# An mLSTM cell and a GELU feed-forward block: the up projection as pairs of 64-row halves of the TensorE array

## The chip, the cores and the metric

The kernel runs on one core of one Trainium2 chip. The metric is the device time of one execution in microseconds. The kernel before took 833.14 us (median of three runs, 832.2 to 833.54).

## What is computed

Two blocks in a row, all in float32 (the two weight matrices arrive in float64). The first is a recurrent cell over 768 tokens for 4 batches of 8 heads with 40 features each:

```python
for t in range(S):
    m_new = np.maximum(f_gate[:, :, t] + m, i_gate[:, :, t])
    f_stab = np.exp(f_gate[:, :, t] + m - m_new)
    i_stab = np.exp(i_gate[:, :, t] - m_new)
    m = m_new
    C = f_stab[..., None, None] * C + i_stab[..., None, None] * np.einsum('bhd,bhe->bhde', vt, kt)
    n = f_stab[..., None] * n + i_stab[..., None] * kt
    y[:, :, t] = sigmoid(o_gate[:, :, t]) * (C q_t) / np.maximum(np.abs(n . q_t), 1.0)
```

Its output, with the heads side by side (3072 tokens of 320 features), goes into the second block:

```python
h = x @ w_in                                  # (3072, 320) @ (320, 2048)
g = 0.5 * h * (1.0 + erf(h / sqrt(2)))
return g @ w_out                              # (3072, 2048) @ (2048, 320)
```

## The kernel before

The 768 tokens of a batch are cut into six chunks of 128. For each chunk the kernel runs a **cell stage** (`cell_steps`, line 265) on the four batches, which leaves the 320 features of 4 x 128 = 512 tokens transposed in `xT`, and then an **up stage** (`up_steps`, line 353) that multiplies `xT` by `w_in` and applies GELU. The **down** projection of a chunk (`down_steps`, line 363) is woven into the cell stage of the next chunk, one part of four matmuls after each cell step; the last chunk's runs alone at the end. `weave` (line 23) spreads such filling steps evenly between the steps of the main list, and each engine executes its instructions in the order in which the program issues them.

A cell stage has 16 steps, four per batch: `turn` transposes k and q (tile `pt`, copied out by ScalarE to `kT`, `qT`); `scores` multiplies them (`ps`) and updates the state (`pc`); `values` forms the output `y` on TensorE, VectorE and GpSimd; `turn_y` (line 337) transposes `y`.

*The 320 features* are three blocks of 128, 128 and 64. `turn_y` transposes each block into one tile `px`; VectorE copies two blocks into `xT` (line 342), ScalarE the third (line 343). One up step (one of 16 tiles of 128 columns of `w_in`) is three matmuls over the three blocks, accumulated in one bank `pu`, then one GELU (line 359). A float32 matmul appears in the trace as two passes, so an up stage has 16 x 3 x 2 = 96 passes. A pass of the third block uses 64 of the array's rows, the others 128.

*The heads* of a pair in `scores` (line 286) each use 64 rows, one the lower and one the upper half of the array, with a bank each.

*The weights* come in as bits of float64. `weight_steps` (line 193) cuts `w_in` into 12 pieces (four of 512 columns by three blocks) and `w_out` into 16. `convert` does one on ScalarE (Abs, line 222), GpSimd (lines 223 to 225) and VectorE (lines 227 to 234), and then fetches the piece after the next one. The `w_in` pieces are woven into the first cell stage, the `w_out` pieces into the first up stage.

*Ahead of every cell stage* `activations` (line 257) puts four exponentials and four sigmoids on ScalarE, behind the last GELU; `turn`'s copies stand behind them in the same queue. `distances` (line 246) prepares the exponents on VectorE and GpSimd during the up stage.

PSUM has eight banks here: two each for `tr` (`pt`, `px`), `sc` (`ps`), `h` (`ph`, `pf`, `pc`) and `mm` (`pu`, `po`).

Of the kernel before, what the change touches and what calls it, by code (L numbers as in the profile page):

```python
# [14 lines left out]
P = 128  # L15


# The upper halves of the float64 2^-126 and of the largest below 2^128, read as float32.
TINY = 3.4332275390625e-05
# [3 lines left out]
def weave(main, fill):  # L23
    """Run the steps of main in order with those of fill spread evenly between them."""
    done = 0
    for n, step in enumerate(main):
        step()
        upto = len(fill) * (n + 1) // len(main)
        for f in fill[done:upto]:
            f()  # L30
        done = upto
    for f in fill[done:]:
        f()
# [3 lines left out]
def kernel(  # L37
# [11 lines left out]
):  # L49
    # The cell in chunks of L tokens. With b_t the sum of f from the chunk's first token to t and  # L50
    # a_s = i_s - b_s, the stabiliser is m_t = b_t + M_t, M_t = max(m before the chunk, a_s for s <= t), and
    #   (C_t, n_t) = exp(m_before - M_t) (C, n)_before + sum over s <= t of exp(a_s - M_t) (v_s, 1) k_s^T.
    # Every exponent is at most 0, so this holds for gates of any size.
    nc = tc.nc
# [11 lines left out]
    TG = B * L  # L66
    KX = DM - 2 * P
    NLD = 6
    NM = 3
    WP = 512  # L70
    assert S % L == 0 and DFF % P == 0 and 0 < KX <= P and D <= DP and NLD > B

# [6 lines left out]
    ps_tr = ctx.enter_context(tc.tile_pool(name="ps_tr", bufs=2, space=bass.MemoryType.PSUM))  # L79
    ps_sc = ctx.enter_context(tc.tile_pool(name="ps_sc", bufs=2, space=bass.MemoryType.PSUM))  # L80
    ps_h = ctx.enter_context(tc.tile_pool(name="ps_h", bufs=2, space=bass.MemoryType.PSUM))
    ps_mm = ctx.enter_context(tc.tile_pool(name="ps_mm", bufs=2, space=bass.MemoryType.PSUM))
    gate_ctx = ExitStack()
    gates = gate_ctx.enter_context(tc.tile_pool(name="gates", bufs=1))
    ctx.enter_context(tc.manual_schedule())

    # ---- what stays: weights, state, load buffers with their constant parts
    w_in = const.tile([P, 3, DFF], F32, name="w_in")
    w_out = const.tile([P, NF, DM], F32, name="w_out")
    ident = const.tile([P, P], F32, name="ident")  # L90
    last = const.tile([P, P], F32, name="last")
    xT = const.tile([P, 3, TG], F32, name="xT")
    aT = const.tile([P, NCH, BH], F32, name="aT")
# [12 lines left out]
    def load(n):  # L106
        """The inputs of token tile n (chunk n // B of batch n % B), one token a partition."""
        if n >= NCH * B:
            return
        c, b = divmod(n, B)  # L110
        for src, dst in ((q, qb), (k, kb), (v, vb), (o_gate, ob)):
            nc.sync.dma_start(out=dst[n % NLD][:, :, 0:D],
                              in_=src[b, :, c * L:(c + 1) * L, :].rearrange("h p d -> p h d"))
# [3 lines left out]
    def load_M(n):  # L117
        """M of token tile n on every partition."""
        if n >= NCH * B:
            return  # L120
        c, b = divmod(n, B)
        Mb[n] = wts.tile([P, H, L], F32, name="Mb", tag="Mb", bufs=NM)
        nc.sync.dma_start(out=Mb[n], in_=M_d[b * H:(b + 1) * H, c * L:(c + 1) * L]
                          .unsqueeze(0).to_broadcast([P, H, L]))
# [19 lines left out]

    # ---- the gates, one row a head
    keep = gates.tile([BH, NCH, L], F32, name="keep")
# [38 lines left out]

    # ---- the weights come in float64: the nearest float32, from the bits
    w_src = {}
# [5 lines left out]
    def weight_steps():  # L193
        """What brings w_in and w_out in, a piece of at most WP columns a step."""
        pieces = []
        for f0 in range(0, DFF, WP):
            for cc, w in enumerate((P, P, KX)):
                pieces.append((w_src["in"][cc * P:cc * P + w, 2 * f0:2 * f0 + 2 * WP], w_in[0:w, cc, f0:f0 + WP]))
        n_in = len(pieces)
        for f in range(NF):  # L200
            pieces.append((w_src["out"][f * P:(f + 1) * P, :], w_out[:, f, :]))
        loaded = {}

        def fetch(i):
            if i < len(pieces):
                src, dst = pieces[i]
                w, n = dst.shape
                t = raw.tile([P, WP, 2], U32, name="bits", tag="bits")
                loaded[i] = t[0:w, 0:n, :]
                nc.sync.dma_start(out=loaded[i].rearrange("p n two -> p (n two)"), in_=src)  # L210

        def convert(i):
            dst = pieces[i][1]
            w, n = dst.shape
            x = loaded.pop(i)
            lo, hi = x[:, :, 0], x[:, :, 1]
            hf = hi.bitcast(F32)
            s = raw.tile([P, WP], F32, name="sig", tag="sig")[0:w, 0:n]
            p = raw.tile([P, WP], F32, name="pow", tag="pow")[0:w, 0:n]
            su, pu = s.bitcast(U32), p.bitcast(U32)  # L220
            # Into the range of float32: 0 below 2^-126, the end of the range from 2^128 on.
            nc.scalar.activation(out=s, in_=hf, func=AF.Abs)  # L222
            nc.gpsimd.tensor_scalar(out=s, in0=s, scalar1=TINY, scalar2=None, op0=OP.is_ge)  # L223
            nc.gpsimd.tensor_tensor(out=s, in0=s, in1=hf, op=OP.mult)  # L224
            nc.gpsimd.tensor_scalar(out=s, in0=s, scalar1=-HUGE, scalar2=HUGE, op0=OP.max, op1=OP.min)  # L225
            # The sign and the power of two, and the 53 bits of the significand rounded to 24.
            nc.vector.tensor_scalar(out=pu, in0=su, scalar1=3, scalar2=0x3F800000,  # L227
                                    op0=OP.logical_shift_left, op1=OP.bitwise_and)
            nc.vector.scalar_tensor_tensor(out=pu, in0=su, scalar=0xC0000000, in1=pu,
                                           op0=OP.bitwise_and, op1=OP.bitwise_or)  # L230
            nc.vector.tensor_scalar(out=su, in0=su, scalar1=0xFFFFF, scalar2=0x100000,
                                    op0=OP.bitwise_and, op1=OP.bitwise_or)
            nc.vector.scalar_tensor_tensor(out=s, in0=lo, scalar=2.0 ** -32, in1=su, op0=OP.mult, op1=OP.add)
            nc.vector.scalar_tensor_tensor(out=dst, in0=s, scalar=2.0 ** -20, in1=p, op0=OP.mult, op1=OP.mult)
            fetch(i + 2)
# [5 lines left out]

    # ---- the cell
    def per_head(t, c, b):
        return t[:, c, b * H:(b + 1) * H].unsqueeze(2)

    def distances(c):
        """M_t - a_s for the chunk's weights exp(a_s - M_t); beyond the diagonal, what gives 0."""
        for b in range(B):
# [16 lines left out]
    def cell_steps(c):  # L265
# [12 lines left out]
        def scores(b):  # L278
            n = c * B + b
            Pm[b] = W.pop(n)  # L280
            # The heads of a pair run side by side in the array: each has its own bank.
            ps = [ps_sc.tile([P, NP, L], F32, name="ps", tag="sc") for hip in range(2)]
            for p in range(NP):
# [33 lines left out]
        def values(b):  # L317
# [7 lines left out]
            else:  # L325
                nc.vector.tensor_copy(out=hs, in_=ph)
            ys[b] = two.tile([P, H, D], F32, name="y", tag="y")
            nc.gpsimd.tensor_tensor(out=ys[b], in0=hs[:, :, 0:D], in1=ob[n % NLD], op=OP.mult)  # L328
            den = two.tile([P, H], F32, name="den", tag="den")
# [3 lines left out]
            nc.vector.reciprocal(out=den, in_=den)  # L333
            nc.vector.tensor_tensor(out=ys[b], in0=ys[b], in1=den.unsqueeze(2).to_broadcast([P, H, D]), op=OP.mult)
            load(n + NLD)

        def turn_y(b):
            y = ys[b].rearrange("p h d -> p (h d)")
            px = ps_tr.tile([P, 3, L], F32, name="px", tag="tr")
            for cc, w in enumerate((P, P, KX)):  # L340
                nc.tensor.transpose(px[0:w, cc, :], y[:, cc * P:cc * P + w], ident)  # L341
            nc.vector.tensor_copy(out=xT[:, 0:2, b * L:(b + 1) * L], in_=px[:, 0:2, :])
            nc.scalar.copy(out=xT[0:KX, 2, b * L:(b + 1) * L], in_=px[0:KX, 2, :])

# [6 lines left out]

    # ---- the feed-forward block, on the tokens of one chunk of every batch
    def up_steps(g):
        def step(f):
            m = slice(f * P, (f + 1) * P)
            pu = ps_mm.tile([P, TG], F32, name="pu", tag="mm")
            for cc, w in enumerate((P, P, KX)):
                nc.tensor.matmul(pu, w_in[0:w, cc, m], xT[0:w, cc, :], start=(cc == 0), stop=(cc == 2))  # L358
            nc.scalar.activation(out=g[:, f, :], in_=pu, func=AF.Gelu)  # L359

        return [lambda f=f: step(f) for f in range(NF)]

# [62 lines left out]
```

## Time and profile before

| | |
|---|---|
| Median of three runs | 833.14 us |
| Span of the profiled execution | 830.5 us |
| TensorE matmul busy | 674.7 us (81%) |
| VectorE, ScalarE, GpSimd busy | 240.7, 170.4, 199.5 us |
| Mean granted TensorE clock | 0.910 |
| One up stage, chunks 1 to 5 | 47.3 us |

The span runs from the first to the last instruction; the 2.6 us between it and the median of the runs lie outside of the profile. The matmul busy time counts passes whose ends are modelled and overlap, so a busy TensorE says where the engine has work, not how fast it could be. The rate is read from the starts of passes that follow each other.

### The profile page before, as it was taken

How to read it: one execution, taken by the hardware profiler on the slowest of the kernel's cores; microseconds unless marked ns; L12 is line 12 of the kernel's file. 1: busy time of each engine (PE TensorE's matmuls, PEld its weight loads, DVE VectorE, ACT ScalarE, POOL GpSimd, SP SyncE). 2: the span in 40 equal slices, each digit the busy share in tenths (PEclk: the TensorE clock that was granted, in tenths of full speed). 3: DMA queues.
4: the chain of work that ended last, by engine and by line, in shares of the span. 5: the costliest groups of instructions: out<-in, count | busy, mean ns of one | idle time of the engine just before them, and what ended most of it. 6: DMA issues, size and time to landing. Idle time of an engine off the chain costs nothing.

```text
span 830.5 us, 7094 instructions
## 1 busy us (share of the span) xinstructions
PE 674.7 (81%) x2714; PEld 394.8 (48%) x2714; DVE 240.7 (29%) x438; ACT 170.4 (21%) x288; POOL 199.5 (24%) x214
## 2 busy tenths in 40 slices
PE   2136424477579999799999799997999997999998
PEld 1125321122258733388533587333885335773365
DVE  4257554455534320034400144200344001330000
ACT  1411002111330022510223300225102234012200
POOL 2276654766612130011300021300113000000000
PEclk9975556788879999999999899998999998999999
DMA  9944371522204540024500035400221000000000
GB/s 141 248 80 95 66 120 29 148 64 63 63 9 66 79 110 0 0 41 66 133 23 1 6 64 82 109 0 1 41 40 41 1 0 9 9 17 0 0 9 24
DMA packets 132208, 43.47 MB, mean 52 GB/s; under 512 B 101104, under 2 KB 128752, under 8 KB 132176
## 3 DMA queue, kind: packets, MB, share of 16 engines
q1 hardware_dynamic: 132176, 43.04, 25.7%
q8 instruction: 21, 0.34, 0.2%
q14 instruction: 11, 0.09, 0.0%
HBM read 38.99 MB, written 4.03 MB: 52 GB/s over the span
## 4 chain that ended last, share of the span: by engine, by line
PE 67%; POOL 13%; issue 11%; ACT 5%; DVE 1%; DMA 1%; SPq 0%; POOLq 0%; ACTq 0%
PE pu L358 28%; PE po L371 25%; POOL sig L225 4%; PE ph L321 4%; POOL sig L223 4%; POOL sig L224 3%; PE ps L286 3%; PE pf L293 3%; ACT W L260 2%; PE pt L273 2%; PE pc L305 2%; POOL W L253 1%; ACT ob L263 1%; PE px L341 1%; ACT L263 1%
## 5 line engine op out<-in xcount | busy, mean ns | idle before, releaser
L358 PE MATMUL pu<-xT,w_in 128*128 128x512 f32 (+1 forms) x576 | 296.2, 646 | 36.4 <-ACT g L359 20.8
L371 PE MATMUL po<-w_out,g 128*128 128x320 f32 x768 | 228.5, 445 | 0.0
L358 PEld LDWEIGHTS pu<-xT,w_in 128*128 128x128 f32 (+1 forms) x576 | 96.6, 193 | 233.2 <-issue 189.8
L371 PEld LDWEIGHTS po<-w_out,g 128*128 128x128 f32 x768 | 143.6, 196 | 51.2 <-issue 5.0
L289 DVE TENSOR_TENSOR W<-ps,W 128x512 f32<-128x512 f32 x48 | 30.9, 685 | 293.5 <-PE ps L286 293.5
L359 ACT ACTIVATE g<-pu 128x512 f32<-128x512 f32 x96 | 57.1, 594 | 187.2 <-PE pu L358 187.2
L314 POOL TENSOR_TENSOR state<-state,dec 64x164 f32<-64x164 f32 x32 | 14.7, 461 | 241.5 <-PE pf L293 240.3
L273 PE MATMUL pt<-ident,kb 128*128 128x128 f32 x96 | 19.2, 335 | 60.5 <-ACT kT L276 60.5
L328 POOL TENSOR_TENSOR y<-hs,ob 128x320 f32<-128x320 f32 x24 | 19.3, 805 | 189.0 <-DVE hs L324 164.8
L321 PEld LDWEIGHTS ph<-vb,W 128*128 128x128 f32 x384 | 53.0, 215 | 4.0 <-PE px L341 0.8
L321 PE MATMUL ph<-vb,W 128*128 128x41 f32 x384 | 51.7, 300 | 0.4 <-PE px L341 0.4
L305 PE MATMUL pc<-vw,kb 128*128 128x82 f32 x160 | 24.9, 306 | 32.2 <-POOL vw L300 32.2
L253 POOL TENSOR_SCALAR_AFFINE_SELECT W<-W 128x1024 f32<-128x1024 f32 x24 | 37.2, 1571 | 56.9 <-DVE W L251 56.9
L273 PEld LDWEIGHTS pt<-ident,kb 128*128 128x128 f32 x96 | 14.1, 173 | 69.3 <-ACT kT L276 63.5
L223 POOL TENSOR_SCALAR sig<-sig 128x320 f32<-128x320 f32 (+2 forms) x28 | 34.8, 1243 | 47.0 <-ACT sig L222 47.0
L225 POOL TENSOR_SCALAR sig<-sig 128x320 f32<-128x320 f32 (+2 forms) x28 | 44.3, 1582 | 2.5
L251 DVE TENSOR_TENSOR W<-Mb,aT 128x1024 f32<-128x1024 f32 x24 | 33.3, 1425 | 26.0 <-DMA Mb<-M_d 26.0
L227 DVE TENSOR_SCALAR pow<-sig 128x320 uint32<-128x320 uint32 (+2 forms) x28 | 15.2, 543 | 86.3 <-POOL sig L225 86.2
L305 PEld LDWEIGHTS pc<-vw,kb 128*128 128x128 f32 x160 | 22.7, 219 | 33.3 <-POOL vw L300 33.3
L374 ACT COPY o_sb<-po 128x320 f32<-128x320 f32 x24 | 10.2, 425 | 132.3 <-PE po L371 132.3
L276 ACT COPY kT<-pt 128x512 f32<-128x512 f32 x24 | 13.9, 579 | 106.5 <-PE pt L273 106.5
L222 ACT ACTIVATE sig<-bits 128x320 f32<-128x320 f32 (+2 forms) x28 | 15.6, 563 | 97.4 <-DMA bits<-in_moe_w_out_dram 66.3
(71 smaller groups left out, 453.9 us busy)
## 6 DMA issues: line engine op xcount, KB each, us to landing
Mb<-M_d SPq DMA_DIRECT2D x24, 512.0 KB, 5.3
bits<-in_moe_w_out_dram SPq DMA_DIRECT2D x16, 320.0 KB, 2.9
bits<-in_moe_w_in_dram SPq DMA_DIRECT2D x8, 512.0 KB, 3.8
qb<-in_q_dram SPq DMA_DIRECT2D x24, 160.0 KB, 4.1
kb<-in_k_dram SPq DMA_DIRECT2D x24, 160.0 KB, 4.2
vb<-in_v_dram SPq DMA_DIRECT2D x24, 160.0 KB, 4.2
ob<-in_o_gate_dram SPq DMA_DIRECT2D x24, 160.0 KB, 3.8
out_dram<-o_sb SPq DMA_DIRECT2D x24, 160.0 KB, 1.9
```

The costliest lines, as they stand in the source:

```text
L223: nc.gpsimd.tensor_scalar(out=s, in0=s, scalar1=TINY, scalar2=None, op0=OP.is_ge)
L224: nc.gpsimd.tensor_tensor(out=s, in0=s, in1=hf, op=OP.mult)
L225: nc.gpsimd.tensor_scalar(out=s, in0=s, scalar1=-HUGE, scalar2=HUGE, op0=OP.max, op1=OP.min)
L251: nc.vector.tensor_tensor(out=W[n], in0=Mb.pop(n), in1=per_head(aT, c, b).to_broadcast([P, H, L]), op=OP.subtract)
L253: nc.gpsimd.affine_select(out=W[n], in_=W[n], compare_op=OP.is_ge, fill=1.0e4, base=0, pattern=[[0, H], [1, L]], channel_multiplier=-1)
L273: nc.tensor.transpose(pt[:, p, :], src[n % NLD][:, 2 * p:2 * p + 2, :].rearrange("p h d -> p (h d)"), ident)
L289: nc.vector.tensor_tensor(out=w, in0=ps[hip], in1=w, op=OP.mult)
L305: nc.tensor.matmul(pc[:, p, :], kb[n % NLD][:, m, :].rearrange("p h d -> p (h d)"), vw[:, m, :].rearrange("p h d -> p (h d)"), start=True, ...
L321: nc.tensor.matmul(ph[:, h, :], Pm[b][:, h, :], vb[n % NLD][:, h, :], start=True, stop=True)
L358: nc.tensor.matmul(pu, w_in[0:w, cc, m], xT[0:w, cc, :], start=(cc == 0), stop=(cc == 2))
L359: nc.scalar.activation(out=g[:, f, :], in_=pu, func=AF.Gelu)
L371: nc.tensor.matmul(po, g[:, f, b * L:(b + 1) * L], w_out[:, f, :], start=(f == 0), stop=(f == NF - 1))
```

## The change

The 320 features become five blocks of 64. Two up tiles are done at a time, as a pair: the even tile's five matmuls use the lower 64 rows of the array, the odd tile's the upper 64, in turn, each into a bank of its own. For that the rows of `w_in` are laid out anew: a piece now holds one block of 64 rows, for even tiles on partitions 0 to 63 and for odd ones on 64 to 127, so there are ten pieces of 128 partitions and each is fetched by two DMAs. `xT` needs every block on both halves of the partitions: `y` is extended by a copy of its first 64 columns (a new VectorE copy), and `turn_y` makes five transposes of 128 columns at a step of 64, in two tiles `px`, so that block k lands on the lower and block k + 1 on the upper partitions. VectorE copies the lower halves, ScalarE the upper ones, two copies each. The pool of `ps` is dissolved; `ps`, `pu` and `po` share four banks.

```diff
+    R = P // 2
+    NK = DM // R
-    ps_sc = ctx.enter_context(tc.tile_pool(name="ps_sc", bufs=2, space=bass.MemoryType.PSUM))
-    ps_mm = ctx.enter_context(tc.tile_pool(name="ps_mm", bufs=2, space=bass.MemoryType.PSUM))
+    ps_mm = ctx.enter_context(tc.tile_pool(name="ps_mm", bufs=4, space=bass.MemoryType.PSUM))
-    w_in = const.tile([P, 3, DFF], F32, name="w_in")
+    w_in = const.tile([P, NK, DFF // 2], F32, name="w_in")
-    xT = const.tile([P, 3, TG], F32, name="xT")
+    xT = const.tile([P, NK, TG], F32, name="xT")
...
-        for f0 in range(0, DFF, WP):
-            for cc, w in enumerate((P, P, KX)):
-                pieces.append((w_src["in"][cc * P:cc * P + w, 2 * f0:2 * f0 + 2 * WP], w_in[0:w, cc, f0:f0 + WP]))
+        for f0 in range(0, DFF, 2 * WP):
+            for k in range(NK):
+                src = w_src["in"][k * R:(k + 1) * R, 2 * f0:2 * (f0 + 2 * WP)]
+                src = src.rearrange("k (m two x) -> k m two x", two=2, x=2 * P)
+                pieces.append(([(slice(R * e, R * e + R), src[:, :, e, :]) for e in range(2)],
+                               w_in[:, k, f0 // 2:f0 // 2 + WP]))
...
-                nc.sync.dma_start(out=loaded[i].rearrange("p n two -> p (n two)"), in_=src)
+                for r, src in parts:
+                    to = loaded[i][r].rearrange("p n two -> p (n two)")
+                    if len(src.shape) == 3:
+                        to = to.rearrange("p (m x) -> p m x", x=2 * P)
+                    nc.sync.dma_start(out=to, in_=src)
...
-            ps = [ps_sc.tile([P, NP, L], F32, name="ps", tag="sc") for hip in range(2)]
+            ps = [ps_mm.tile([P, NP, L], F32, name="ps", tag="mm") for hip in range(2)]
...
-            ys[b] = two.tile([P, H, D], F32, name="y", tag="y")
+            ys[b] = two.tile([P, DM + R], F32, name="y", tag="y")
...
+            nc.vector.tensor_copy(out=ys[b][:, DM:DM + R], in_=ys[b][:, 0:R])
...
-            px = ps_tr.tile([P, 3, L], F32, name="px", tag="tr")
-            for cc, w in enumerate((P, P, KX)):
-                nc.tensor.transpose(px[0:w, cc, :], y[:, cc * P:cc * P + w], ident)
-            nc.vector.tensor_copy(out=xT[:, 0:2, b * L:(b + 1) * L], in_=px[:, 0:2, :])
-            nc.scalar.copy(out=xT[0:KX, 2, b * L:(b + 1) * L], in_=px[0:KX, 2, :])
+            for k0, n in ((0, 3), (3, 2)):
+                px = ps_tr.tile([P, n, L], F32, name="px", tag="tr")
+                for k in range(n):
+                    nc.tensor.transpose(px[:, k, :], ys[b][:, (k0 + k) * R:(k0 + k + 2) * R], ident)
+                t = slice(b * L, (b + 1) * L)
+                nc.vector.tensor_copy(out=xT[0:R, k0:k0 + n, t], in_=px[0:R])
+                nc.scalar.copy(out=xT[R:P, k0:k0 + n, t], in_=px[R:P])
...
-            m = slice(f * P, (f + 1) * P)
-            pu = ps_mm.tile([P, TG], F32, name="pu", tag="mm")
-            for cc, w in enumerate((P, P, KX)):
-                nc.tensor.matmul(pu, w_in[0:w, cc, m], xT[0:w, cc, :], start=(cc == 0), stop=(cc == 2))
-            nc.scalar.activation(out=g[:, f, :], in_=pu, func=AF.Gelu)
+            pu = [ps_mm.tile([P, TG], F32, name="pu", tag="mm") for e in range(2)]
+            for k in range(NK):
+                for e in range(2):
+                    r = slice(R * e, R * e + R)
+                    nc.tensor.matmul(pu[e], w_in[r, k, f // 2 * P:(f // 2 + 1) * P], xT[r, (k - e) % NK, :],
+                                     start=(k == 0), stop=(k == NK - 1))
+            for e in range(2):
+                nc.scalar.activation(out=g[:, f + e, :], in_=pu[e], func=AF.Gelu)
-        return [lambda f=f: step(f) for f in range(NF)]
+        return [lambda f=f: step(f) for f in range(0, NF, 2)]
```

TensorE at the end of the cell stage of chunk 1, from the last `turn_y` into the up stage, before (`px` are the transposes of `y`, `po` a down part, `pu` the up matmuls; what stands in brackets are the engines that a row waits for):

```order
L341 MATMUL px<-ident,y 128x128 [waits DVE_49,Activation_49]
L341 MATMUL px<-ident,y 128x128
L341 MATMUL px<-ident,y 64x128
L371 MATMUL po<-w_out,g 128x320 x4
L358 MATMUL pu<-xT,w_in 128x512 [waits DVE_49]
L358 MATMUL pu<-xT,w_in 128x512
L358 MATMUL pu<-xT,w_in 128x512 [waits Activation_49] x2
```

The same place in the changed kernel:

```order
L356 MATMUL px<-ident,y 128x128 [waits Activation_49]
L356 MATMUL px<-ident,y 128x128 x2
L356 MATMUL px<-ident,y 128x128 [waits Activation_49]
L356 MATMUL px<-ident,y 128x128
L392 MATMUL po<-w_out,g 128x320 x4
L377 MATMUL pu<-xT,w_in 128x512 [waits DVE_49]
L377 MATMUL pu<-xT,w_in 128x512 [waits Activation_49]
L377 MATMUL pu<-xT,w_in 128x512 x4
```

Two transposes more stand in the step, the two `px` tiles each wait for ScalarE, and the second up matmul (the first on the upper half) waits for ScalarE, whose copy into `xT` it reads.

ScalarE in the first cell stage, before (`sig<-bits` is the Abs that begins the conversion of a piece, `kT` and `qT` are the copies of `turn`):

```order
L222 ACTIVATE sig<-bits 128x512 [waits DMAHW2_49]
L222 ACTIVATE sig<-bits 128x512 [waits DMAHW3_49]
L276 COPY kT<-pt 128x512 [waits PE_49,Activation_49]
L276 COPY qT<-pt 128x512 [waits PE_49,Activation_49]
L222 ACTIVATE sig<-bits 64x512 [waits DMAHW4_49,DVE_49]
```

The same place in the changed kernel:

```order
L233 ACTIVATE sig<-bits 128x512 [waits DMAHW3_49,DMAHW2_49]
L287 COPY kT<-pt 128x512 [waits PE_49,Activation_49]
L287 COPY qT<-pt 128x512 [waits PE_49,Activation_49]
L233 ACTIVATE sig<-bits 128x512 [waits DMAHW5_49,DMAHW4_49]
L233 ACTIVATE sig<-bits 128x512 [waits DMAHW7_49,DMAHW6_49,DVE_49]
```

With ten pieces instead of twelve spread over the 16 steps, the second piece's Abs has moved behind the copies of the third `turn`.

## Rows read from the trace of the kernel before

**Rows 1.** The page: the chain that ended last, shares of the span by engine.

```profile
PE 67%; POOL 13%; issue 11%; ACT 5%; DVE 1%; DMA 1%; SPq 0%; POOLq 0%; ACTq 0%
```

**Rows 2.** Busy us by engine in two stretches: chunk 2's and chunk 0's up stage.

```profile
core 0: us, PE busy (x) PEld busy (x) DVE busy (x) ACT busy (x) POOL busy (x), PEclk, DMA share, GB/s
405.40:452.60 47.20, 47.20 (x97) 15.29 (x95) 3.78 (x3) 10.66 (x17) 6.35 (x5) 1.00 0.17 48
...
142.00:226.00 84.00, 56.38 (x104) 18.61 (x102) 45.09 (x80) 15.99 (x31) 54.78 (x50) 0.83 0.29 84
```

**Rows 3.** The chain in order of time (start us, us, what): an up stage, last down.

```profile
405.36 47.28 PE pu L358 x96
...
792.61 34.66 PE po L371 x128
```

**Rows 4.** Timeline, TensorE: starts of five successive passes inside chunk 2's up stage.

```profile
429.79 1.02 PE L358 MATMUL pu<-xT,w_in 128*128 128x512 f32 x2
...
430.22 1.22 PE L358 MATMUL pu<-xT,w_in 128*128 128x512 f32 x2
...
430.74 1.12 PE L358 MATMUL pu<-xT,w_in 64*128 64x512 f32 x2
...
431.27 1.22 PE L358 MATMUL pu<-xT,w_in 64*128 64x512 f32 x2
...
431.79 1.13 PE L358 MATMUL pu<-xT,w_in 128*128 128x512 f32 x2
```

**Rows 5.** Timeline, TensorE: a scores step (64-row halves in turn) and transposes.

```profile
467.50 1.16 PE L286 MATMUL ps<-qT,kT 64*128 64x128 f32 x16
468.59 1.12 PE L293 MATMUL pf<-state,qT 128*128 128x82 f32 x8
...
472.64 0.60 PE L273 MATMUL pt<-ident,kb 128*128 128x128 f32 x4
473.07 0.60 PE L273 MATMUL pt<-ident,qb 128*128 128x128 f32 x4
```

**Rows 6.** Timeline, all engines: the last turn_y and the next up stage's start.

```profile
517.92 2.32 PE L371 MATMUL po<-w_out,g 128*128 128x320 f32 x8
...
518.58 0.26 ACT L343 COPY xT<-px 64x128 f32<-64x128 f32 x1 [2.23 <-DVE xT L342]
...
520.08 3.56 PE L358 MATMUL pu<-xT,w_in 128*128 128x512 f32 x7
```

**Rows 7.** Timeline, all engines: from an up stage's end into the cell stage.

```profile
452.67 0.60 ACT L359 ACTIVATE g<-pu 128x512 f32<-128x512 f32 x1 [2.37 <-PE pu L358]
453.28 1.28 ACT L260 ACT_TABLE_LOAD   x1
...
461.85 1.11 PE L273 MATMUL pt<-ident,kb 128*128 128x128 f32 x4 [6.04 <-ACT kT L276]
```

**Rows 8.** Timeline, all engines: conversions of w_in pieces in the first cell stage.

```profile
46.70 1.67 POOL L223 TENSOR_SCALAR sig<-sig 128x512 f32<-128x512 f32 x1
...
50.58 0.58 ACT L276 COPY qT<-pt 128x512 f32<-128x512 f32 x1 [0.26 <-PE pt L273]
...
118.57 1.50 POOL L223 TENSOR_SCALAR sig<-sig 128x512 f32<-128x512 f32 x1
...
125.84 0.69 DVE L234 SCALAR_TENSOR_TENSOR w_in<-sig,pow 128x512 f32<-128x512 f32 x1
...
126.45 0.41 DVE L342 COPY xT<-px 128x256 f32<-128x256 f32 x1
...
127.80 1.49 POOL L223 TENSOR_SCALAR sig<-sig 128x512 f32<-128x512 f32 x1 [4.36 <-ACT sig L222]
...
144.26 0.68 DVE L234 SCALAR_TENSOR_TENSOR w_in<-sig,pow 64x512 f32<-64x512 f32 x1
```

**Rows 9.** Timeline: one round of two w_out pieces in chunk 0's up stage.

```profile
203.00 9.30 PE L358 MATMUL pu<-xT,w_in 128*128 128x512 f32 x12 [2.13 <-ACT g L359]
...
211.95 0.49 ACT L222 ACTIVATE sig<-bits 128x320 f32<-128x320 f32 x1 [6.72 <-DMA bits<-in_moe_w_out_dram]
```

More of the change, by code (lines that the diff above doesn't have):

```diff
@@ L66 @@
     TG = B * L
-    KX = DM - 2 * P
+    R = P // 2
+    NK = DM // R
     NLD = 6
@@ L70 @@
     WP = 512
-    assert S % L == 0 and DFF % P == 0 and 0 < KX <= P and D <= DP and NLD > B
+    assert S % L == 0 and DFF % (2 * P) == 0 and DM % R == 0 and D <= DP and NLD > B
     const = ctx.enter_context(tc.tile_pool(name="const", bufs=1))
@@ L195, in weight_steps @@
         pieces = []
-        for f0 in range(0, DFF, WP):
-            for cc, w in enumerate((P, P, KX)):
-                pieces.append((w_src["in"][cc * P:cc * P + w, 2 * f0:2 * f0 + 2 * WP], w_in[0:w, cc, f0:f0 + WP]))
+        for f0 in range(0, DFF, 2 * WP):
[4 more added lines that the diff above has]
+                               w_in[:, k, f0 // 2:f0 // 2 + WP]))
         n_in = len(pieces)
         for f in range(NF):
-            pieces.append((w_src["out"][f * P:(f + 1) * P, :], w_out[:, f, :]))
+            pieces.append(([(slice(0, P), w_src["out"][f * P:(f + 1) * P, :])], w_out[:, f, :]))
         loaded = {}
@@ L205, in fetch @@
             if i < len(pieces):
-                src, dst = pieces[i]
-                w, n = dst.shape
+                parts, dst = pieces[i]
+                n = dst.shape[1]
                 t = raw.tile([P, WP, 2], U32, name="bits", tag="bits")
-                loaded[i] = t[0:w, 0:n, :]
-                nc.sync.dma_start(out=loaded[i].rearrange("p n two -> p (n two)"), in_=src)
+                loaded[i] = t[:, 0:n, :]
+                for r, src in parts:
[3 more added lines that the diff above has]
+                    nc.sync.dma_start(out=to, in_=src)
         def convert(i):
             dst = pieces[i][1]
-            w, n = dst.shape
+            n = dst.shape[1]
             x = loaded.pop(i)
@@ L217, in convert @@
             hf = hi.bitcast(F32)
-            s = raw.tile([P, WP], F32, name="sig", tag="sig")[0:w, 0:n]
-            p = raw.tile([P, WP], F32, name="pow", tag="pow")[0:w, 0:n]
+            s = raw.tile([P, WP], F32, name="sig", tag="sig")[:, 0:n]
+            p = raw.tile([P, WP], F32, name="pow", tag="pow")[:, 0:n]
             su, pu = s.bitcast(U32), p.bitcast(U32)
@@ L326, in values @@
                 nc.vector.tensor_copy(out=hs, in_=ph)
-            ys[b] = two.tile([P, H, D], F32, name="y", tag="y")
-            nc.gpsimd.tensor_tensor(out=ys[b], in0=hs[:, :, 0:D], in1=ob[n % NLD], op=OP.mult)
+            ys[b] = two.tile([P, DM + R], F32, name="y", tag="y")
+            y = ys[b][:, 0:DM].rearrange("p (h d) -> p h d", d=D)
+            nc.gpsimd.tensor_tensor(out=y, in0=hs[:, :, 0:D], in1=ob[n % NLD], op=OP.mult)
             den = two.tile([P, H], F32, name="den", tag="den")
@@ L333, in values @@
             nc.vector.reciprocal(out=den, in_=den)
-            nc.vector.tensor_tensor(out=ys[b], in0=ys[b], in1=den.unsqueeze(2).to_broadcast([P, H, D]), op=OP.mult)
+            nc.vector.tensor_tensor(out=y, in0=y, in1=den.unsqueeze(2).to_broadcast([P, H, D]), op=OP.mult)
+            nc.vector.tensor_copy(out=ys[b][:, DM:DM + R], in_=ys[b][:, 0:R])
             load(n + NLD)
         def turn_y(b):
-            y = ys[b].rearrange("p h d -> p (h d)")
-            px = ps_tr.tile([P, 3, L], F32, name="px", tag="tr")
-            for cc, w in enumerate((P, P, KX)):
-                nc.tensor.transpose(px[0:w, cc, :], y[:, cc * P:cc * P + w], ident)
-            nc.vector.tensor_copy(out=xT[:, 0:2, b * L:(b + 1) * L], in_=px[:, 0:2, :])
-            nc.scalar.copy(out=xT[0:KX, 2, b * L:(b + 1) * L], in_=px[0:KX, 2, :])
+            for k0, n in ((0, 3), (3, 2)):
[5 more added lines that the diff above has]
+                nc.scalar.copy(out=xT[R:P, k0:k0 + n, t], in_=px[R:P])
         steps = []
```

## The prediction

> **What bounds the kernel now.** I began with the chain of work that ended last: two thirds of the span are TensorE passes [rows 1], and in order of time they are, in chunks 1 to 5, an up stage of 96 passes in 47.28 us between cell stages in which the passes stand close together too; after the last up stage comes the last down projection [rows 3]. So a pass that becomes shorter in an up stage of chunks 1 to 5 moves the end. ScalarE works 10.66 us of those 47.2 and VectorE less, at a granted clock of 1.00 [rows 2]; they have room. Chunk 0 differs: its up stage lies in 84 us of which GpSimd works 54.78 and TensorE waits [rows 2]. There the conversions of the weights set the time, and a faster TensorE gives nothing.
>
> Next I read the rate inside an up stage, from the starts of passes that follow each other [rows 4]. A 128-row pass starts 0.43 us after the one before (429.79, 430.22). Into the 64-row block, inside it and out of it the steps are 0.52, 0.53 and 0.52 us. Six passes at 0.429 would be 2.57 us; a tile takes 47.28 / 16 = 2.955. So 0.38 us a tile goes where the array changes between 128 and 64 rows, and a 64-row pass of 512 columns costs as much as a full one.
>
> **What halves side by side do.** The only 64-row halves in turn are in the scores: 16 passes of 128 columns, and the next matmul starts 1.09 us after the first of them [rows 5]. Full passes of 128 columns start every 0.43 / 4 = 0.109 us (the transposes, 472.64 to 473.07 [rows 5]), so 16 in a row would be 1.74 us, and eight pairs at once 0.87. The 0.22 over is about one change of rows in and out. The halves do run side by side there, loading their weights too.
>
> **The up stages of chunks 1 to 5.** A pair of tiles is five blocks by two halves by two passes, ten pairs of passes; a stage has 80 pairs. At 0.429 us a pair, as for any pass of 512 columns [rows 4], that is 34.3 us, and 0.2 for the one change of rows at the stage's start: 34.5. Against 47.28 each stage saves 12.8, five save 63.9. Bounds: if I give the start-up of the scores to each pair, 1.09 / 8 = 0.136 against 0.109, a pair of 512 columns takes 0.535 and a stage 42.8; that the halves don't overlap at all is the slow rival. I take 0.429, since the scores' excess has the size of one change of rows and these come once a stage now.
>
> The Trainium skill (TensorE: Matmul & The Clock Gate, section Measured speedup vs the span model) reports that four row tiles of 32 rows with 512 columns gave 3.07 times, not 4. By that share two tiles would give 1.54, an estimate from that page; a pair would take 0.56 us and a stage 44.6, and the kernel would come out near 822 us. The scores show 1.6 with the change of rows in it, and no run here shows 512 columns.
>
> **Behind an up stage.** Exponentials, sigmoids and `turn`'s copies follow the last GELU on ScalarE, and TensorE waits 6.04 us for them [rows 7]. Both tiles of the last pair end together, so two GELUs instead of one stand ahead: +0.60 us [rows 7] at each of four boundaries (chunks 1 to 4; behind chunk 0 an Abs is last, behind chunk 5 the down parts run on), +2.4.
>
> **The cell stages.** `turn_y` has five transposes instead of three: 2 x 0.109 us, four batches, five stages in which TensorE is the chain: +4.4. The copies into `xT` grow: VectorE from one of 256 columns (0.41 us [rows 8]) to two of 384 and 256, ScalarE from one of 128 (0.26 [rows 6]) to two of the same widths, between 0.26 and the 0.58 of 512 columns [rows 8]. ScalarE waits for VectorE's copy before as well [rows 6]. From the first tile's end this is about 0.6 + 0.1 + 0.5 + 0.1 + 0.5 = 1.8 us, an estimate. Ahead of the up stage a down part covers it: 517.92 to 520.08, 2.16 us [rows 6], and the first `px` ends 0.2 earlier still. So 0.5 is left, and I count nothing; without that cover it would be up to 1.8 a stage. VectorE's copy of 64 columns of `y` costs at most the 0.41 of 256 columns and lies behind the same parts. The scores' banks now come from the shared pool: a `ps` can wait for ScalarE's copy of a `po`, but that `po` ended some steps before; nothing again.
>
> **The weights.** A late piece goes round alone: GpSimd from 118.57, VectorE until 125.84 + 0.69 = 126.53, the `xT` copies, Abs, and GpSimd begins the next at 127.80 [rows 8]: 9.23 us a piece. Two pieces fewer would be 18.5 us. But the order changes. The second piece ran directly behind the first, from 46.70; now its Abs stands behind `qT` of the third `turn`, which ended at 50.58 + 0.58 = 51.16 [rows 8], so it begins near 51.9. Further on, fewer pieces run back to back on GpSimd, and each turn of `turn_y` adds some 0.6 of copies. I went through the ten in their new order with the 7.96 us from GpSimd's first to VectorE's last operation, two more where GpSimd goes on to the next piece at once: GpSimd begins at about 41, 52, 57, 68, 74, 88, 100, 110, 123 and 133, and the last `w_in` operation ends near 140.4 instead of 144.94 [rows 8]. I take -4.5, with bounds of -18.5 (all that two pieces take) and 0 (the new order eats it all). Each fetch being two DMAs of shorter runs should hide, since in my walk the bits are there before Abs's turn.
>
> The `w_out` pieces stay 16, in rounds of two whose length is set by fetch, Abs, GpSimd and VectorE. The GELUs, now two by two, fall into the wait of 6.72 us before the next Abs [rows 9], and a pair of tiles at half the clock takes some 8.6 us against a round's 9 to 10. Nothing changes there but the start.
>
> **The sum.** -63.9 + 2.4 + 4.4 - 4.5 = -61.6. The profiled execution's span of 830.5 becomes 768.9; with the 2.6 us that lie outside of it, 771.5 us against the median of 833.14.
>
> **The rivals.** *The reload shows in every pair* (A): the 64-row passes of 512 columns in this trace are 0.53 apart [rows 4], and if that is the half array's own pace and not the change of rows, a stage is 80 x 0.533 = 42.6 us, five save 23.2, and the time is 833.1 - 23.2 + 2.3 = 812. For it: no 64-row pass of that width went faster. Against it: the step into the block is longer by as much, and the scores' passes keep pace. The page's share of 3.07 in 4, told above, would be a milder form of this rival and stands in its chance.
>
> *The halves take turns* (B), so that the change does not do what it says: two streams of 512 columns into two banks might not go at once. Then a stage is 160 x 0.429 = 68.6 us, five lose 106.7, and the time is 942. It decides from a pair of 0.585 us on, where the stage's gain equals the other terms. Against it stand the scores, where two banks take in both halves.
>
> *The covers fail* (C): each `turn_y` waits for its copies, since both tiles `px` now wait for ScalarE, which waits for VectorE, behind `values`. At 1.8 us each, 20 times, that is 36 us, and the time is 807. Against it: between two turns lies at least a down part of 2.16 us [rows 6].
>
> **How the numbers follow.** Forecast 82%, A 8%, B 4%, C 6%. The forecast's own range: down to 757.5 with all 18.5 us of the weights; up by 4.5 if these give nothing, by 4.8 if a pair takes 0.441 (2.5% slower than a lone pass), by 5 for waits of a microsecond in five stages: 786. That holds about eight in ten, and I keep 758 to 786. A measurement of this kernel tells 0.2%, or 1.7 us, from no change. Faster by more takes the forecast, A and C, 95%; slower is B, 4%; 1% is left between.
>
> **What would show it.** The up stages of chunks 1 to 5 should be one run of 160 passes in 34.5 us, starts in twos, 0.43 us apart. 42 to 43 us would be A, over 60 B. Idle time of TensorE ahead of `px` or of the first up matmuls, released by ScalarE's `xT` copy, would be C. The wait behind an up stage should grow from 6.0 to 6.6 us, the last VectorE operation on `w_in` end near 140, and chunk 0's up stage keep its rounds of nearly 10 us. The forecast is wrong above all if the pair's pace is.

## The result, and the profile after

The changed kernel takes 770.16 us (median of four runs, 768.05 to 770.72) against 832.9 us for the kernel before (median of four runs as well). The ratio of the two is 0.9248, with a 95% interval of 0.9231 to 0.9265. The profiled execution has a span of 768.9 us, 61.6 us less than before. The forecast was 771.5 us, with a span of 768.9. In every execution of these runs whose time and span are both on record, 1.7 to 1.9 us lie outside of the span; the 2.6 us that stand ahead and in the forecast also hold the difference between the profiled execution and the median. So the spans are the better comparison.

The chain of work that ended last, in order of time (start us, us, what), shows the up stages of chunks 1, 2 and 5 and the last down projection; these lines answer to [rows 3]:

```profile
289.09 34.58 PE pu L377 x160
...
392.25 34.58 PE pu L377 x160
...
696.55 34.53 PE pu L377 x160
731.08 34.66 PE po L392 x128
```

An up stage has 160 passes instead of 96, and 34.58 us instead of 47.28. The reason stands in the starts of passes inside the stage of chunk 2 (timeline, TensorE: start us, us, what, count of passes that touch a short window):

```profile
399.58 1.02 PE L377 MATMUL pu<-xT,w_in 64*128 64x512 f32 x4
...
400.01 0.60 PE L377 MATMUL pu<-xT,w_in 64*128 64x512 f32 x2
...
400.44 0.60 PE L377 MATMUL pu<-xT,w_in 64*128 64x512 f32 x2
```

Two passes begin together, and the next two 0.43 us later. That is the step that a single 128-row pass had in [rows 4], and the steps of 0.52 and 0.53 are gone. So two 64-row passes of 512 columns, one on each half, cost what one pass of 128 rows costs.

The boundary behind an up stage (timeline of ScalarE and TensorE; brackets: idle before it, and what ended it) answers to [rows 7]:

```profile
426.82 1.08 ACT L380 ACTIVATE g<-pu 128x512 f32<-128x512 f32 x2 [3.21 <-PE pu L377]
427.92 1.28 ACT L271 ACT_TABLE_LOAD   x1
429.21 3.89 ACT L271 ACTIVATE W<-W 128x1024 f32<-128x1024 f32 x4
...
436.49 1.11 PE L284 MATMUL pt<-ident,kb 128*128 128x128 f32 x4 [6.52 <-ACT kT L287]
```

Two GELUs stand before the exponentials where one stood, and TensorE's wait has grown from 6.04 to 6.52 us.

The last `turn_y` of a cell stage answers to [rows 6]:

```profile
389.39 0.71 PE L356 MATMUL px<-ident,y 128*128 128x128 f32 x5
389.92 0.88 DVE L358 COPY xT<-px 64x384 f32<-64x384 f32 x2 [1.82 <-PE px L356]
389.93 2.32 PE L392 MATMUL po<-w_out,g 128*128 128x320 f32 x8
390.50 0.74 ACT L359 COPY xT<-px 64x384 f32<-64x384 f32 x2 [1.96 <-DVE xT L358]
...
392.18 1.56 PE L377 MATMUL pu<-xT,w_in 64*128 64x512 f32 x6
```

ScalarE's second copy ends at 390.50 + 0.74 = 391.24, and the up stage begins at 392.18 without a wait: the down part between them covers the four copies. In chunks 1 to 5 TensorE never waits ahead of `px`; it waits there for ScalarE's copy twice in the first cell stage (6.01 and 11.03 us), where the conversions of the weights set the pace.

In the first cell stage the round of `w_in` pieces is the walk's, 0.5 to 1.3 us late (timeline; these answer to [rows 8]):

```profile
41.34 0.67 ACT L233 ACTIVATE sig<-bits 128x512 f32<-128x512 f32 x1 [0.71 <-DMA bits<-in_moe_w_in_dram]
...
52.76 1.50 POOL L234 TENSOR_SCALAR sig<-sig 128x512 f32<-128x512 f32 x1 [5.09 <-ACT sig L233]
...
133.54 1.50 POOL L234 TENSOR_SCALAR sig<-sig 128x512 f32<-128x512 f32 x1 [5.11 <-ACT sig L233]
...
140.83 0.69 DVE L245 SCALAR_TENSOR_TENSOR w_in<-sig,pow 128x512 f32<-128x512 f32 x1
```

The second piece begins at 52.76 (it was 46.70 before, and about 52 in the walk), the last at 133.54 (walk: 133), and the last operation on `w_in` ends at 141.52 (before 144.94, walk 140.4). The very first Abs now waits 0.71 us for its bits; before it did not. Chunk 0's up stage keeps its rounds: towards its end the first Abs of a round begins at 198.52, 208.30 and 218.06, every 9.8 us.

Term by term, from the starts of the up stages and of chunk 1's first transposes in both chains of work:

| Term | Forecast, us | Measured, us |
|---|---|---|
| Five up stages | -63.9 | -63.5 |
| Weights, up to chunk 1's first transposes (233.31 before, 229.43 after) | -4.5 | -3.9 |
| Cell stage of chunk 1 | +0.9 | +1.4 |
| Four boundaries with the cell stages behind them (chunks 2 to 5) | +5.9 | +4.5 |
| Sum | -61.6 | -61.5 |

That the sum meets the forecast to a tenth is luck: the four terms are off by +0.4, +0.6, +0.5 and -1.4 us.

### The profile page after: what moved, and what is told of

It reads as the page before. It is cut to its first block, busy times and chain, and to the rows that moved or that the text cites. A ratio compares the mean times of both kernels' runs of the same rounds, so it can differ in the third digit from the quotient of the medians.

```text
span 768.9 us, 7997 instructions
## 1 busy us (share of the span) xinstructions
PE 604.9 (79%) x3146; PEld 408.8 (53%) x3146; DVE 247.1 (32%) x476; ACT 177.0 (23%) x310; POOL 189.4 (25%) x208
## 3 DMA queue, kind: packets, MB, share of 16 engines
q1 hardware_dynamic: 136144, 43.04, 28.6%
## 4 chain that ended last, share of the span: by engine, by line
PE 65%; POOL 12%; issue 10%; ACT 6%; DVE 3%; SPq 2%; DMA 2%; POOLq 0%; ACTq 0%; DVEq 0%
PE po L392 27%; PE pu L377 22%; PE ph L332 4%; POOL sig L236 4%; POOL sig L234 3%; POOL sig L235 3%; PE ps L297 3%; PE pf L304 3%; ACT W L271 3%; PE pt L284 2%; SPq L115 2%; PE pc L316 2%; PE px L356 1%; DMA Mb<-M_d 1%; ACT ob L274 1%
## 5 line engine op out<-in xcount | busy, mean ns | idle before, releaser
L377 PE MATMUL pu<-xT,w_in 64*128 64x512 f32 x960 | 217.6, 606 | 28.5 <-ACT g L380 20.4
L377 PEld LDWEIGHTS pu<-xT,w_in 64*128 64x128 f32 x960 | 102.9, 192 | 140.8 <-issue 104.5
L380 ACT ACTIVATE g<-pu 128x512 f32<-128x512 f32 x96 | 51.9, 593 | 129.8 <-PE pu L377 129.8
L359 ACT COPY xT<-px 64x384 f32<-64x384 f32 (+1 forms) x48 | 17.9, 420 | 118.1 <-DVE xT L358 118.1
L234 POOL TENSOR_SCALAR sig<-sig 128x320 f32<-128x320 f32 (+1 forms) x26 | 31.5, 1212 | 52.4 <-ACT sig L233 52.4
L238 DVE TENSOR_SCALAR pow<-sig 128x320 uint32<-128x320 uint32 (+1 forms) x26 | 14.0, 538 | 86.3 <-POOL sig L236 86.2
L236 POOL TENSOR_SCALAR sig<-sig 128x320 f32<-128x320 f32 (+1 forms) x26 | 40.4, 1555 | 2.3
L262 DVE TENSOR_TENSOR W<-Mb,aT 128x1024 f32<-128x1024 f32 x24 | 30.9, 1321 | 28.8 <-DMA Mb<-M_d 28.8
L395 ACT COPY o_sb<-po 128x320 f32<-128x320 f32 x24 | 10.2, 425 | 127.5 <-PE po L392 122.0
```

Source lines behind the costliest of these rows:

```text
L262: nc.vector.tensor_tensor(out=W[n], in0=Mb.pop(n), in1=per_head(aT, c, b).to_broadcast([P, H, L]), op=OP.subtract)
L377: nc.tensor.matmul(pu[e], w_in[r, k, f // 2 * P:(f // 2 + 1) * P], xT[r, (k - e) % NK, :], start=(k == 0), stop=(k == NK - 1))
L380: nc.scalar.activation(out=g[:, f + e, :], in_=pu[e], func=AF.Gelu)
```

## Experiments

Each experiment is an edit of the changed kernel, but for the second, which is one of the kernel before. Beside the first four runs the kernel before took 831.5 us, beside the last three 831.85. The changed kernel's 770.16 us was measured beside 832.9, so a microsecond or so in a difference to it means nothing. Where one time is given it is a single run.

**1. The halves one after the other.** Does the gain come from neighbours in the instruction stream that use different halves?

```diff
-            for k in range(NK):
-                for e in range(2):
+            for e in range(2):
+                for k in range(NK):
```

> The changed kernel with the ten matmuls of a pair in another order: first the five blocks of the lower half, then the five of the upper half. Work and row changes are the same; only neighbours no longer use different halves, except where one half's last pass meets the other's first. If the halves running side by side is what makes a pair take 4.3 us, a pair now needs 18 places of 0.429 us (20 less the two where the halves meet), an up stage 61.8 us instead of 34.6, five stages 136 us more: about 906 us; without any overlap 68.6 us and 940 us. The rival, that TensorE finds the overlap whatever the order, expects 770 us.

It took 818.52 us. The chain of work shows each up stage at

```profile
399.94 44.77 PE pu L377 x160
```

So the order does matter, by 10.2 us a stage, but neither expectation held: a stage of eight pairs takes 104 places of 0.429 us, 13 a pair, not 18 or 20. The starts of the passes at that stage's beginning show why (us; the lower half's ten passes and the upper half's first five, told apart by the order of the program):

```
lower  399.87 400.40 400.83 401.26 401.69 402.12 402.55 402.98 403.40 403.83
upper                                             402.55 403.09 403.51 403.94 404.37
```

The upper half's first pass begins together with the lower half's seventh, when three of the lower half's passes, which stand before it in the program, have not begun. TensorE runs a half's passes in order, but lets the other half begin up to three passes early. The trace goes on like this: each half's first pass begins together with the other's seventh, 2.69 us after the other's first. That is six places and 0.1 us for a half's longer first step (399.87 to 400.40, 402.55 to 403.09).

**2. The change of rows alone.** The kernel before, with zeros that fill the third block up to 128 rows.

```diff
+    nc.gpsimd.memset(w_in[KX:P, 2, :], 0.0)
+    nc.gpsimd.memset(xT[KX:P, 2, :], 0.0)
-                nc.tensor.matmul(pu, w_in[0:w, cc, m], xT[0:w, cc, :], start=(cc == 0), stop=(cc == 2))
+                nc.tensor.matmul(pu, w_in[:, cc, m], xT[:, cc, :], start=(cc == 0), stop=(cc == 2))
```

> The kernel before, with the third block of 64 features padded by zeros to 128 rows (64 zero rows in the weights and in the transposed input), so that an up stage never changes between 128 and 64 rows. Still 96 passes. My theory, that 0.38 us a tile goes to the change of rows, expects an up stage of 96 x 0.429 = 41.2 us instead of 47.28 and, over five stages, 30.5 us less than the kernel before: about 802 us. The rival, that a 64-row pass is slow by itself or that the loss lies between the tiles, expects something between 802 and 833; that the change of rows is nearly all of the gain expects 770.

It took 804.35 us, 27 less than the kernel before beside it; the five up stages themselves gave the 30 expected (the chain of work):

```profile
399.80 41.21 PE pu L360 x96
```

96 passes at 0.429 us, no more. About 3.5 of the 30 go back in the four later cell stages, whose first down parts are longer here (3.96 to 4.14 us; 2.61 to 3.77 before).

Padding takes away the change of rows and the 64-row passes together, so by itself this run can't tell which of them was slow. Experiment 1 can: there the lower half's passes run alone from 400.40 to 402.55, and they stand 0.43 us apart. A 64-row pass is not slow by itself. So of the 12.7 us that an up stage became shorter by the change, 6.1 were the change between 128 and 64 rows, which adding zeros removes as well, and 6.6 are the pairing: 80 places instead of 96.

**3. The pieces in their old places.** What were two pieces fewer worth, and what did their new order take?

```diff
-    weave(cell_steps(0), in_steps)
+    weave(cell_steps(0), in_steps + [lambda: None] * 2)
```

> The changed kernel, with the ten pieces of w_in at the places that the first ten had in the kernel before (the filling list ends with two empty steps), so that the second piece runs directly behind the first. My theory is that two pieces fewer were worth 18 us and that their new order gave 14 of them back. It expects the last VectorE operation on w_in to end near 127 to 129 us instead of 141, and about 758 us. The rival, that the fetch in two DMAs or the copies into xT set the pace of the stage, expects 768 to 771, no difference.

It took 761.2 us (ratio to the kernel before 0.9153, 0.9138 to 0.9168), 9 less than the changed kernel; the spans of the two profiled executions differ by 7.4. In its timeline the second piece runs behind the first again, and the last ends earlier:

```profile
47.10 1.67 POOL L234 TENSOR_SCALAR sig<-sig 128x512 f32<-128x512 f32 x1
...
130.03 0.69 DVE L245 SCALAR_TENSOR_TENSOR w_in<-sig,pow 128x512 f32<-128x512 f32 x1
...
132.68 0.88 DVE L358 COPY xT<-px 64x384 f32<-64x384 f32 x2 [1.17 <-PE px L356]
...
133.49 3.48 DVE L262 TENSOR_TENSOR W<-Mb,aT 128x1024 f32<-128x1024 f32 x3
```

The theory's sign holds and its size does not: `w_in` is ready 10.8 us sooner (130.72 against 141.52), not 12 to 14, and chunk 1's first transposes come 7.7 us sooner (221.75 against 229.43). Behind the last piece there now stands the last turn of `y`, and behind its copies VectorE prepares the next chunk's exponents: from 133.49 on, where it was 141.44 in the changed kernel. The 10.8 us have become 8.0 there.

**4. ScalarE's work for the next chunk inside the up stage.** Is it what TensorE waits for behind an up stage?

```diff
+        ups = up_steps(g)
+        if 0 < c < NCH - 1:
+            ups.insert(4, lambda c=c: activations(c + 1))
-        weave(up_steps(g), out_steps if c == 0 else [])
+        weave(ups, out_steps if c == 0 else [])
         if c + 1 < NCH:
-            activations(c + 1)
+            if c == 0:
+                activations(c + 1)
```

> The changed kernel, with the exponentials and sigmoids of the next chunk on ScalarE in the middle of the up stage (after four of eight pairs) in chunks 1 to 4, instead of behind the last GELU. My theory of the boundary, that TensorE's 6.5 us wait and the halved clock behind it come from that ScalarE work alone, expects the wait to shrink to under 1 us, ScalarE's block of 9.3 us to stop TensorE for about 2.5 us in the stage, and some 6 us less in each of four chunks: about 746 us. The rival, that the stall only moves into the up stage, expects 768 to 771.

It took 753.88 us (0.9072, 0.9049 to 0.9096): 16 less than the changed kernel where 24 were expected. The wait behind the stage is gone, and so is the slow first down part (2.15 or 2.16 us behind each of these stages). But inside the stage this appears:

```profile
415.04 1.28 ACT L380 ACT_TABLE_LOAD   x1
416.33 2.06 ACT L380 ACTIVATE g<-pu 128x512 f32<-128x512 f32 x4
...
416.98 11.03 PE L377 MATMUL pu<-xT,w_in 64*128 64x512 f32 x40 [2.56 <-ACT g L380]
```

TensorE stops for 2.56 us, as expected. Then 40 passes (20 places) take 11.0 us instead of 8.6. The granted clock (PEclk) is 0.96 over the stage, where the changed kernel's stage has 1.00, and 0.66 over the 5 us behind the stop:

```profile
core 0: us, PE busy (x) PEld busy (x) DVE busy (x) ACT busy (x) POOL busy (x), PEclk, DMA share, GB/s
388.50:428.00 39.50, 36.94 (x161) 17.27 (x161) 3.15 (x3) 17.64 (x27) 6.75 (x5) 0.96 0.21 58
...
417.00:422.00 5.00, 5.00 (x15) 2.83 (x17) 0.00 (x0) 1.40 (x3) 0.00 (x0) 0.66 0.00 0
```

Four steps of each half, from 418.4 to 421.8 us, are 0.85 us long, twice the 0.429; that is 1.7 of the 2.4 us over. The rest is mostly that the halves don't start together behind the stop (416.98 and 417.47). The stage takes 39.5 us (40.7 in chunk 1). The miss is this second cost: a stop inside the stage costs the clock behind it as well.

**5. Every transpose of `y` twice.** Do the two more transposes of a turn lie on the path?

```diff
-                for k in range(n):
+                for k in [*range(n)] * 2:
```

> The changed kernel with each of the five transposes of a turn of y done twice into the same place (the second time over the first). My theory, that a transpose there costs its 0.109 us on the path in the five cell stages that carry a down projection and nothing in the first, expects 5 x 0.109 x 4 x 5 = 10.9 us more, about 781 us. If the transposes lay in slack of TensorE (as they would where it waited for copies), the rival, there would be no change; if the covers of the copies into xT had little left, it would be more than 11 us.

It took 784.1 us, a span of 782.3, that is 13.4 more than the changed kernel's. The doubled turn stands without a wait between its neighbours (timeline, TensorE):

```profile
488.22 1.26 PE L356 MATMUL px<-ident,y 128*128 128x128 f32 x10
489.31 2.32 PE L392 MATMUL po<-w_out,g 128*128 128x320 f32 x8
```

Ten transposes hold the next part up by 1.09 us, 0.109 each. The 10.9 us are there; of the 2.5 over, 1.1 arose before chunk 1's first transposes and 1.3 in the first down parts of the five cell stages, whose time varies (below): 17.5 us together instead of 16.2.

**6. Both early edits, with ScalarE's block in two.** A version drawn from runs 3 and 4: the exponentials after the fourth pair, the sigmoids after the sixth.

```diff
+            ups.insert(6, lambda c=c: sigmoids(c + 1))
+            ups.insert(4, lambda c=c: exponentials(c + 1))
```

> The changed kernel with both earlier edits, and ScalarE's work for the next chunk cut in two: the exponentials after the fourth pair of an up stage, the sigmoids after the sixth. In the run with one block of 9.3 us TensorE stopped for 2.6 us and then ran at a lower clock, so that the up stage took 39.5 us instead of 34.6. My theory is that TensorE is two pairs (8.6 us) ahead of the GELUs, so blocks of 6.5 and 4.1 us stop it nowhere; then the stage keeps 34.6 us, and the time is 753.9 - 9 - 4 x 4.9 = about 725 us. If TensorE still stops for each block, the rival, it is 740 to 750.

It took 729.81 us (0.8776, 0.8761 to 0.8791), the fastest of all. The chain of work shows the stage nearly whole again:

```profile
374.73 34.99 PE pu L379 x159
```

Blocks of 6.5 and 4.1 us stop TensorE for 0.4 us a stage at most, and the period from one up stage to the next, chunks 1 to 4, is 94.7 us (it was 102.6 to 103.2 in the changed kernel). The forecast was 725, so it took 4.8 us more. The spans of experiment 4 and of this run differ by 27.4 us where 28.6 were expected: the pieces gave 7.5 us, not 9. The rest of the miss is that experiment 4's profiled execution was 3.1 us longer than the median from which the forecast counts; where those 3.1 us lie no run tells.

**7. The halves in turn by two blocks.** Is the look-ahead of experiment 1 real?

```diff
-            for k in range(NK):
-                for e in range(2):
+            for e, k in [(e, k) for ks in ((0, 1), (2, 3), (4,)) for e in range(2) for k in ks]:
```

> The changed kernel with the halves in turn by two blocks, not by one: four passes of the lower half, four of the upper, four and four, two and two. With all ten of one half first, the other half began when three passes of the first had not yet started. If TensorE really hands out passes up to three ahead of the one that runs in the same half, four passes of one half don't hold up the other, an up stage stays at 34.6 us, and the time at about 770 us. If that overlap came from something else, such as a bank coming free, and a pass only meets its direct neighbour, three of four passes run alone: a pair takes 15 to 16 places of 0.429 us, a stage some 52 to 55 us, and the time is about 860.

It took 767.93 us, with each up stage at 34.5 us:

```profile
492.44 34.54 PE pu L377 x159
```

The lower half's first pass begins at 492.37 and the upper's first at 492.38, though three passes of the lower half that stand ahead of it have not begun. So four passes of one half ahead of the other's cost nothing, as experiment 1's reading says, and the rival, that a pass only meets its direct neighbour, falls. What sets the number three no run tells.

## Why the prediction was right

*The pace of a pair.* This carried the forecast, and it was right: 0.429 us, and 34.58 us a stage where 34.5 was said. The evidence was 128 columns wide in the scores; at 512 columns the two streams into two banks go on side by side. Rival A (0.53 us a pair) falls with the profile after, and so does B; experiment 1 shows that even halves in the wrong order don't fall back to taking turns, and that 64-row passes on one half keep a step of 0.43 us, which speaks against A as well. The Trainium skill's 3.07 for four row tiles (TensorE: Matmul & The Clock Gate, section Measured speedup vs the span model) does not carry over to two of 64 rows: here the pairs keep the full factor of two.

*Where the old time went.* The 0.38 us a tile at the change of rows was right, shown by experiment 2: it is half of the gain of an up stage, and zeros would have taken it without any pairing. The steps that the prediction names, 0.52, 0.53 and 0.52, hold only 0.28 of it. There is a fourth: behind the first pass of 128 rows, which starts at 431.79, the next starts at 432.32 (timeline of the kernel before, TensorE).

```profile
432.32 0.59 PE L358 MATMUL pu<-xT,w_in 128*128 128x512 f32 x1
```

*The boundary.* Two GELUs for one were to cost 0.6 us each time; the wait grew by 0.48, since two GELUs in a row take 1.08 us and one alone 0.60. Experiment 4 shows that the wait comes from ScalarE's work for the next chunk: with that moved, it is gone.

*The cell stages.* The transposes cost 0.109 us each on the path (experiment 5), as said. With the boundaries the four later cell stages came to +4.5 instead of +5.9. Some 0.6 of the difference is the boundaries, and 0.7 the first long down part behind the wait: in the chains of work its eight passes took 2.61, 3.75, 2.65 and 3.77 us before and these after,

```profile
335.30 3.41 PE po L392 x8
...
438.45 3.04 PE po L392 x8
...
541.24 2.85 PE po L392 x8
...
643.83 2.75 PE po L392 x8
```

a sum of 12.05 against 12.78. These parts follow the granted clock: in the 3 us from their start it is 0.87, 0.50, 0.86 and 0.50 before and 0.60, 0.72, 0.79 and 0.82 after. Why the clock comes back sooner in one chunk and later in another no run tells.

*The covers.* They held, with 0.9 us left before the up stage (0.5 was said); rival C did not come about in chunks 1 to 5.

*The weights.* The walk through the new order was the part with the widest bounds (0 to -18.5), and it gave -4.5 where -3.9 was measured. Its last start, 133, and its 7.96 us give 141.0 for the end of `w_in`, not the 140.4 that the prediction took; measured were 141.52. What else it missed is that the fetch in two DMAs does not quite hide: the first Abs waits 0.71 us for bits, and the row of pieces stands late from there on. The wait differs between executions. In the runs of experiments 1, 4 and 7, whose first cell stage is the same program, it is 0, 0.39 and 0.46 us, and `w_in` ends at 140.97, 141.05 and 141.46; chunk 1's first transposes begin at 229.21, 228.45 and 229.57. The term's miss of 0.6 us is no larger than this scatter. The two profiles with the old fetch (before and experiment 2) show no such wait; that shorter runs are the cause was not tried by itself.

Experiment 3 shows what the count gave and what the order took back. In their old places the ten pieces end `w_in` 14.2 us sooner than the kernel before (130.72 against 144.94), in the new order 3.4. So two pieces fewer were worth 14.2 us all in all, not 18.5, and the order took 10.8 of them.

## What to carry to other kernels

The block of 64 rows that was left of the contraction cost twice here: for half an empty array, and for the change of rows on either side. Read the second cost from the starts of passes, since busy time hides it; filling up with zeros saved that one, and pairing two outputs on the two halves saved both. When a change also alters the number of filling steps, follow the whole new order on every engine before counting the steps that are gone as time gained.

## What the runs showed of the hardware

Two 64-row passes of 512 float32 columns, one on each half and into a bank each, start together and are followed by the next two after 0.429 us, the step of one full pass. The description of the kernel before says that each engine executes its instructions in the order of the program. For TensorE's passes on different halves that is not so: a half's pass began while three earlier passes of the other half had not (experiment 1), and four passes of one half ahead of the other's cost nothing (experiment 7). Leaving a stretch of 128-row passes for two 64-row ones and coming back cost 0.38 us (experiment 2), while 64-row passes on one half alone kept a step of 0.43 us (experiment 1). A stop of 2.56 us in the middle of an up stage was followed by a granted clock of 0.66 over 5 us, and 20 places behind it took 11.0 us instead of 8.6 (experiment 4).
